# PV with V stationary and two heads on array columns, denominators from added chunks of P, gate logits in the output transposes, deeper page loads

## The chip, the cores and the metric

The kernel runs on one core of a Trainium2 chip. The metric is device time in microseconds (us) of one execution; lower is better. The engines are TensorE (PE, with its weight loads listed apart as PEld), VectorE (DVE), ScalarE (ACT), GpSimd (POOL) and SyncE (SP), which here only issues DMA transfers. TensorE multiplies a stationary operand, loaded first, with columns of a moving operand that stream past it; its clock has two levels, 1.2 and 2.4 GHz.

## What is computed

A causal attention in blocks of 64 over 8 batches, 8 heads, 576 positions and head size 64, and then a mixture of experts without dropped tokens: each of the 4608 tokens goes to the one expert of eight with the largest gate logit.

```
scores = q @ k.T / sqrt(64), kept where block(i) >= block(j)       # blocks of 64
attn   = exp(scores - max) / (sum(exp(...)) + 1e-9)
x      = (attn @ v) as [4608 tokens, 512]
logits = x @ w_gate;  e = argmax(logits);  g = softmax(logits)[e]
y      = g * (relu(x @ w1[e]) @ w2[e])          # w1: 512x1024, w2: 1024x512
```

## The kernel before

**Attention.** The 64 heads are worked off as 32 pairs (p; the loop at L361). A pair's q and k are loaded two pairs ahead (`load`, L123, on SP's queue, together with v), cast to fp16 on POOL (`cast`, L143), transposed on PE (`trans`, L151) and copied out by DVE. `scores` (L165) makes the scores transposed, key positions on partitions and query positions along the columns: four chunks of 128 key rows and one of 64, in steps t = 0 to 3, the two heads on the two halves of the array's rows. ACT takes the exponential from PSUM into the fp32 tile `pt`, called P below; POOL clears the corner that the mask excludes (L189, L191).

`attend` (L193) is the product with V, called PV. For each head and each block i of 128 query rows, every chunk c up to i gives one matmul: the 128 columns of P are stationary, and V's 64 columns and a column of ones (65 in all) move. The column of ones gives the softmax's denominator. That is 15 fp32 matmuls per head; each fp32 matmul is two weight loads and two matmul instructions in the trace, so a pair has 60. `normalise` (L210) divides on DVE, POOL casts the result into the fp16 row `x16`; `xtrans` (L233) transposes the fp32 result on PE, DVE copies it, and `logits` (L243) multiplies it with the gate weights `wg`, 8 columns wide; DVE adds the logits of the four pairs of a batch.

After each batch, `route` (L256) picks the expert on DVE, computes a slot for each token and scatters the rows with five indirect DMAs from POOL (L335) into `xsorted`, a DRAM buffer of 43 pages of 128 rows. It has been filled with empty rows by one DMA of 5.5 MB (L352). The experts' weights `wall` come in 16 loads from POOL's queue (`load_weights`, L91).

**Pages.** The second loop (L473) takes page after page: `mload` loads its rows (L415, SP's queue, tile `xs`, four buffers, two pages ahead), `mtx` transposes (L424), `m1` multiplies with w1 (L438), ACT takes the relu, `mth` transposes (L450), `m2` multiplies with w2 (L460), ACT scales (L463), and POOL scatters the rows to the output with an indirect DMA (L464) that reads its indices from `xs`. So a buffer of `xs` is free when that scatter is through.

**Order.** PE and ACT run in the order of the code (`manual_schedule`); for DVE, POOL and SP a scheduler fixes the order when the program is built. Each queue works in its order: an instruction that waits holds up all behind it.

Of the kernel before, what the change touches and what calls it, by code (L numbers as in the profile page):

```python
# [17 lines left out]
ROW = 258  # L18
# [4 lines left out]
def kernel(  # L23
# [37 lines left out]
    wg = consts.tile([128, HP, E], F32)  # L61
    nc.sync.dma_start(out=wg, in_=moe_w_gate.rearrange("(do di) e -> di do e", di=128))
# [27 lines left out]

    def load_weights(n):  # L91
        e, part = n // 2, n % 2
        if part == 0:
            nc.gpsimd.dma_start(
                out=wall[:, e, 0:8, :].rearrange("p (c a) f -> p c (a f)", c=4),
                in_=moe_w1[e].rearrange("(c p) f -> p c f", p=128))
        else:
            nc.gpsimd.dma_start(
                out=wall[:, e, 8:16, :],
                in_=moe_w2[e].rearrange("(c p) d -> p c d", p=128))  # L100

    with tc.tile_pool(name="ld", bufs=2) as ld, \
         tc.tile_pool(name="vp", bufs=1) as vp, \
# [4 lines left out]
         tc.tile_pool(name="s_ps", bufs=4, space=bass.MemoryType.PSUM) as s_ps, \  # L108
         tc.tile_pool(name="o_ps", bufs=2, space=bass.MemoryType.PSUM) as o_ps, \
         tc.tile_pool(name="t_ps", bufs=2, space=bass.MemoryType.PSUM) as t_ps:  # L110
        vts = [vp.tile([128, 5, 2, 65], F32, name=f"v{i}") for i in range(3)]
        for t in vts:
            nc.gpsimd.memset(t[:, :, :, 64:65], 1.0)
        xTs = [vp.tile([128, 640], F32, name=f"xT{i}") for i in range(2)]
        for t in xTs:
            nc.gpsimd.memset(t[:, 576:640], 0.0)
        ohs = [vp.tile([128, 5, E], F16, name=f"oh{i}") for i in range(2)]
# [5 lines left out]
        def load(p):  # L123
            b, h0 = p // HP, 2 * (p % HP)
            qk = ld.tile([128, 2, 5, 128], F32, name="qk32")
            vt = vts[p % 3]
            for n, src in ((0, q), (1, k)):
                for h in range(2):
                    nc.sync.dma_start(
                        out=qk[:, n, 0:4, h * 64:h * 64 + 64],  # L130
                        in_=src[b, h0 + h, 0:512, :].rearrange("(c p) d -> p c d", p=128))
                nc.sync.dma_start(
                    out=qk[0:64, n, 4, :].rearrange("p (h d) -> p h d", h=2),
                    in_=src[b, h0:h0 + 2, 512:576, :].rearrange("h p d -> p h d"))
            for h in range(2):
                nc.sync.dma_start(
                    out=vt[:, 0:4, h, 0:64],
                    in_=v[b, h0 + h, 0:512, :].rearrange("(c p) d -> p c d", p=128))
                nc.sync.dma_start(out=vt[h * 64:h * 64 + 64, 4, h, 0:64],
                                  in_=v[b, h0 + h, 512:576, :])  # L140
            st["qk", p] = qk

        def cast(p):  # L143
            qk = st.pop(("qk", p))
            h16 = c16.tile([128, 2, 5, 128], F16, name="qk16")
            nc.gpsimd.tensor_copy(h16[:, :, 0:4, :].rearrange("p n c d -> p n (c d)"),  # L146
                                  qk[:, :, 0:4, :].rearrange("p n c d -> p n (c d)"))
            nc.gpsimd.tensor_copy(h16[0:64, :, 4, :], qk[0:64, :, 4, :])
            st["qk16", p] = h16

        def trans(p, n):  # L151
            h16 = st["qk16", p]
            if n == 0:
                st["qkT", p] = c16.tile([128, 2, 576], F16, name="qkT")
            ps = t_ps.tile([128, 576], F16, name="tp")
            for c in range(4):
                nc.tensor.transpose(ps[:, c * 128:c * 128 + 128], h16[:, n, c, :], ident16)  # L157
            nc.tensor.transpose(ps[:, 512:576], h16[0:64, n, 4, :], ident16[0:64, 0:64])
            nc.vector.tensor_copy(st["qkT", p][:, n, :], ps)  # L159


        SC = (((0, 0, 0, 512),), ((1, 0, 128, 448), (0, 448, 512, 64)),
              ((2, 0, 256, 320), (3, 320, 384, 192)))

        def scores(p, t):  # L165
            qkT = st["qkT", p]
            if t == 0:
                st["pt", p] = ptp.tile([128, 2 * 1536 + 64], F32, name="pt")
            pt = st["pt", p]
            if t == 3:  # L170
                sp = s_ps.tile([128, 64], F32, name="s")
                for h in range(2):
                    r = slice(h * 64, h * 64 + 64)
                    nc.tensor.matmul(out=sp[r, :], lhsT=qkT[r, 1, 512:576],
                                     rhs=qkT[r, 0, 512:576], start=True, stop=True)
                nc.scalar.activation(pt[:, 3072:3136], sp, AF.Exp, scale=scale)
                return
            sps = [s_ps.tile([128, 512], F32, name="s") for _ in range(2)]
            for n, (c, o, q0, w) in enumerate(SC[t]):
                for h in range(2):  # L180
                    r = slice(h * 64, h * 64 + 64)
                    nc.tensor.matmul(out=sps[h][:, o:o + w],  # L182
                                     lhsT=qkT[r, 1, c * 128:c * 128 + 128],
                                     rhs=qkT[r, 0, q0:q0 + w], start=True, stop=True)
            for h in range(2):
                o = h * 1536 + t * 512
                nc.scalar.activation(pt[:, o:o + 512], sps[h], AF.Exp, scale=scale)  # L187
            two = pt[64:128, 0:3072].rearrange("p (h w) -> p h w", h=2)
            nc.gpsimd.memset(two[:, :, t * 512:t * 512 + 64], 0.0)  # L189
            if t == 2:  # L190
                nc.gpsimd.memset(two[:, :, 1344:1408], 0.0)  # L191

        def attend(p, h, i):  # L193
            pt, vt = st["pt", p], vts[p % 3]
            if i == 0:
                st["o", p, h] = o_ps.tile([128, 5, 65], F32, name="o")
            o = st["o", p, h]
            m = 128 if i < 4 else 64
            for c in range(i + 1):
                if c == 4:  # L200
                    r, col = slice(h * 64, h * 64 + 64), 3072
                else:
                    r = slice(0, 128)
# [310 lines left out]
```

## Time and profile before

| what | us |
|---|---|
| median of 3 runs (1133.26 to 1137.33) | 1134.91 |
| the profiled execution | 1133.68 |
| its span, first to last instruction | 1131.9 |
| PE busy | 855.7 |
| PE's weight loads busy | 621.7 |
| DVE, ACT, POOL busy | 197.3, 187.8, 193.3 |

The span is the time between the first and the last instruction of the profiled execution; 1.8 us of its time lie outside. Busy times are sums over stages that differ, and a busy PE is not PE at full rate: matmuls overlap, and their rows say how long each was in the array. PE does half its busy time in one line, L206, the product with V. In the second part, the pages, PE is busy for 251 of 424 us.

### The profile page before, as it was taken

What the parts mean: (1) busy time and instruction counts of PE and PEld (TensorE: products, weight loads), DVE (VectorE), ACT (ScalarE), POOL (GpSimd) and SP (SyncE); (2) the same over time, 40 slices, a digit from 0 to 9 for tenths busy, and PEclk for the clock granted to TensorE, in tenths of its full rate; (3) what the DMA queues carried; (4) which work ended last, traced back from release to release, by engine and by line L of the source; (5) the groups of instructions that cost most, each with busy time, mean ns of one, the idle gap of its engine ahead of it and who ended that gap; (6) DMA issues with size and microseconds to landing.
All of it is one profiled execution on the core that took longest, in us unless ns stands there. A gap on an engine that the chain in (4) does not pass through costs nothing. (4 is left out here: it accounts for less than half of the span.)

```text
span 1131.9 us, 12146 instructions
## 1 busy us (share of the span) xinstructions
PE 855.7 (76%) x4357; PEld 621.7 (55%) x4357; DVE 197.3 (17%) x769; ACT 187.8 (17%) x319; POOL 193.3 (17%) x392
## 2 busy tenths in 40 slices
PE   2319999999999999999999991655566555566555
PEld 1217888787888888887878791332232222232222
DVE  0001132131131221311311312111011110111110
ACT  1001121111111121211111100211111111111111
POOL 3112223122122121221131211001110011110011
PEclk9999999999999999999999999988888888888778
DMA  9999952222222121222220000111111111100110
GB/s 186 232 205 186 159 101 69 57 64 63 55 52 70 37 66 45 54 62 49 57 49 17 20 8 28 32 37 42 38 38 33 38 42 43 41 33 31 42 41 5
DMA packets 145785, 71.46 MB, mean 63 GB/s; under 512 B 118976, under 2 KB 138176, under 8 KB 145728
## 3 DMA queue, kind: packets, MB, share of 16 engines
q1 hardware_dynamic: 127952, 39.71, 15.3%
q0 software_dynamic: 17776, 30.98, 12.3%
q8 instruction: 37, 0.61, 0.2%
q14 instruction: 20, 0.16, 0.0%
HBM read 67.56 MB, written 21.71 MB: 79 GB/s over the span
## 5 line engine op out<-in xcount | busy, mean ns | idle before, releaser
L206 PE MATMUL o<-v,pt 128*128 128x65 f32 (+2 forms) x1920 | 399.8, 391 | 0.0
L206 PEld LDWEIGHTS o<-v,pt 128*128 128x128 f32 (+2 forms) x1920 | 360.9, 292 | 56.3 <-issue 33.8
L187 ACT ACTIVATE pt<-s 128x512 f32<-128x512 f32 x192 | 104.0, 595 | 419.8 <-PE s L182 419.8
L424 PE MATMUL xps<-ident,xs 128*128 128x128 f16 x172 | 19.5, 244 | 178.9 <-DMA xs<-xsorted 159.6
L460 PE MATMUL yp<-wall,hT 128*128 x344 | 132.7, 557 | 0.0
L424 PEld LDWEIGHTS <-xs 128*128 128x128 f16 x172 | 11.3, 106 | 199.4 <-DMA xs<-xsorted 197.4
L464 POOL DMA_INDIRECT out_dram<-y,xs x43 | 42.3, 985 | 379.4 <-ACT y L463 377.6
L438 PE MATMUL hp<-wall,xsT 128*128 x344 | 87.2, 399 | 2.6 <-DVE xsT L427 2.6
L157 PE MATMUL tp<-ident,qk 128*128 128x128 f16 x256 | 39.0, 308 | 63.0 <-POOL qk L146 63.0
L427 DVE COPY xsT<-xps 128x512 f16<-128x512 f16 x43 | 18.3, 425 | 366.1 <-PE xps L424 366.1
L460 PEld LDWEIGHTS <-hT 128*128 128x128 f16 x344 | 45.0, 136 | 62.2 <-issue 55.5
L463 ACT ACTIVATE y<-yp,xs 128x512 f32<-128x512 f32 x43 | 29.6, 687 | 285.1 <-PE yp L460 285.1
L182 PE MATMUL s<-qkT 64*128 64x512 f16 (+4 forms) x320 | 63.9, 447 | 16.2 <-DVE qkT L159 15.9
L248 PEld LDWEIGHTS tp<-wg,xT 128*128 128x128 f32 x320 | 72.1, 333 | 0.7 <-DVE xT L238 0.7
L248 PE MATMUL tp<-wg,xT 128*128 128x8 f32 x320 | 71.9, 357 | 0.5 <-DVE xT L238 0.5
L219 DVE RECIPROCAL rec<-o 128x4 f32<-128x4 f32 (+1 forms) x128 | 21.3, 166 | 290.5 <-PE o L206 290.5
L146 POOL CAST qk<-qk 128x1024 f16<-128x1024 f32 x32 | 33.2, 1037 | 197.4 <-issue 140.4
L438 PEld LDWEIGHTS <-xsT 128*128 128x128 f16 x344 | 36.3, 106 | 53.4 <-issue 20.0
L157 PEld LDWEIGHTS <-qk 128*128 128x128 f16 x256 | 22.2, 132 | 68.8 <-POOL qk L146 63.3
L443 ACT ACTIVATE h<-hp 128x1024 f16<-128x1024 f32 x43 | 44.0, 1024 | 78.9 <-PE hp L438 78.9
L189 POOL MEMSET pt<- 64x128 f32 x96 | 19.2, 201 | 215.9 <-ACT pt L187 214.5
L335 POOL DMA_INDIRECT xsorted<-x,slot x40 | 39.0, 974 | 33.1 <-DMA xsorted<-x,slot 17.2
(95 smaller groups left out, 460.7 us busy)
## 6 DMA issues: line engine op xcount, KB each, us to landing
wall<-in_moe_w_dram POOLq DMA_DIRECT2D x16, 1024.0 KB, 13.0
qk<-in_q_dram SPq DMA_DIRECT2D x64, 128.0 KB, 2.6
qk<-in_k_dram SPq DMA_DIRECT2D x64, 128.0 KB, 2.8
v<-in_v_dram SPq DMA_DIRECT2D x64, 128.0 KB, 2.3
xsorted<-fill SPq DMA_DIRECT2D x1, 5547.0 KB, 52.0
xs<-xsorted SPq DMA_DIRECT2D x43, 129.0 KB, 2.0
qk<-in_q_dram SPq DMA_DIRECT2D x32, 32.0 KB, 2.4
qk<-in_k_dram SPq DMA_DIRECT2D x32, 32.0 KB, 2.5
```

What stands on the lines that cost most here:

```text
L146: nc.gpsimd.tensor_copy(h16[:, :, 0:4, :].rearrange("p n c d -> p n (c d)"), qk[:, :, 0:4, :].rearrange("p n c d -> p n (c d)"))
L157: nc.tensor.transpose(ps[:, c * 128:c * 128 + 128], h16[:, n, c, :], ident16)
L182: nc.tensor.matmul(out=sps[h][:, o:o + w], lhsT=qkT[r, 1, c * 128:c * 128 + 128], rhs=qkT[r, 0, q0:q0 + w], start=True, stop=True)
L187: nc.scalar.activation(pt[:, o:o + 512], sps[h], AF.Exp, scale=scale)
L206: nc.tensor.matmul(out=o[0:m, i, :], lhsT=pt[r, col:col + m], rhs=vt[r, c, h, :], start=(c == 0), stop=(c == i), skip_group_check=True)
L248: nc.tensor.matmul(out=lp[:, i * E:i * E + E], lhsT=xT[:, i * 128:i * 128 + 128], rhs=wg[:, hp, :], start=True, stop=True)
L335: nc.gpsimd.indirect_dma_start(out=xsorted[:, :], out_offset=bass.IndirectOffsetOnAxis(ap=slot[0:m, j:j + 1], axis=0), in_=x16[0:m, j, :], ...
L424: nc.tensor.transpose(ps[:, c * 128:c * 128 + 128], pg["xs", T].bitcast(F16)[:, c * 128:c * 128 + 128], ident16)
L438: nc.tensor.matmul(out=hp[:, half * 512:half * 512 + 512], lhsT=xT[:, c * 128:c * 128 + 128], rhs=weight(T, 2 * c + half), start=(c == 0), ...
L443: nc.scalar.activation(h, hp, AF.Relu)
L460: nc.tensor.matmul(out=yp, lhsT=hT[:, f * 128:f * 128 + 128], rhs=weight(T, 8 + f), start=(f == 0), stop=(f == 7))
L464: nc.gpsimd.indirect_dma_start(out=out[:, :], out_offset=bass.IndirectOffsetOnAxis(ap=xs[:, 257:258], axis=0), in_=y, in_offset=None, boun ...
```

## The change

PV is turned round. `attend` now holds a chunk of V (128 keys by 64) and lets P move, in two column ranges of the query positions, 0 to 255 and 256 to 575. The result is transposed: head 0's 64 output dimensions on PSUM partitions 0 to 63, head 1's on 64 to 127, so the two heads' products use the left and the right half of the array's columns. A pair has 14 such matmuls (28 instructions); DVE copies the two ranges into `oT`.

The column of ones is gone. `sums` adds the chunks of P on POOL into `acc`, five adds per pair; `denominators` multiplies 32 columns of ones with P's first 128 columns and with `acc`, each result on its own 32 partitions, and DVE copies them into `den` in four pieces.

`finish` replaces `xtrans`, `logits` and POOL's casts: with a 128-column block of `oT` stationary, one matmul against `wgi`, an identity with the gate weights beside it (144 columns), gives the transposed output and the gate logits; five small matmuls with `den` stationary turn the denominators. DVE divides both straight into `x16` and a logits tile that `route` sums. `finish` for a pair runs one pass later, so the loop has one pass more.

Loads of q and k become two DMAs of 1 KB pieces instead of four of 256 B pieces; v is loaded one pair ahead; the fill of the empty rows is cut into eight pieces, one per batch (12 pages first, then 4 or 5). In the pages, `xs` gets eight buffers and the loads run four pages ahead. In PSUM the scores take two tiles of two banks instead of four of one, and ACT's exponential covers both heads at once. The fp16 tile `qk16` has one buffer instead of two.

```diff
-                nc.tensor.matmul(out=o[0:m, i, :], lhsT=pt[r, col:col + m],
-                                 rhs=vt[r, c, h, :], start=(c == 0), stop=(c == i),
-                                 skip_group_check=True)
...
+        def sums(p):
+
+            pt, p4 = st["pt", p]
+            acc = op.tile([128, 2, 448], F32, name="acc")
+            nc.gpsimd.tensor_tensor(out=acc, in0=pt[:, :, 128:576], in1=pt[:, :, 576:1024],
+                                    op=ALU.add)
+            nc.gpsimd.tensor_tensor(out=acc[:, :, 128:448], in0=acc[:, :, 128:448],
+                                    in1=pt[:, :, 1024:1344], op=ALU.add)
+            nc.gpsimd.tensor_tensor(out=acc[:, :, 256:448], in0=acc[:, :, 256:448],
+                                    in1=pt[:, :, 1344:1536], op=ALU.add)
...
+        def attend(p, cs, half):
...
+            lo, hi = ((0, 256), (256, 576))[half]
...
+            for c in cs:
+                q0 = max(lo, 128 * c)
+                for h in range(2):
+                    r = slice(0, 128) if c < 4 else slice(h * 64, h * 64 + 64)
+                    src = p4[r, :] if c == 4 else \
+                        pt[:, h, COL[c] + q0 - 128 * c:COL[c] + hi - 128 * c]
+                    nc.tensor.matmul(out=o[h * 64:h * 64 + 64, q0 - lo:hi - lo],
+                                     lhsT=vt[r, c, h, :], rhs=src,
+                                     start=(c == 0), stop=(c == last), skip_group_check=True)
+            if cs[-1] == last:
+                nc.vector.tensor_copy(oTs[p % 2][:, lo:hi], st.pop(("o", p, half)))
+
+        def denominators(p):
...
+            ps = t_ps.tile([128, 320], F32, name="tp")
+            for part in range(2):
+                for h in range(2):
+                    r = slice(h * 64, h * 64 + 32)
+                    src = acc[:, h, 0:128] if part else pt[:, h, 0:128]
+                    nc.tensor.matmul(out=ps[r, part * 128:part * 128 + 128], lhsT=ones32,
+                                     rhs=src, start=True, stop=True, skip_group_check=True)
+                    if part == 0:
+                        r = slice(h * 64 + 32, h * 64 + 64)
+                        nc.tensor.matmul(out=ps[r, :], lhsT=ones32, rhs=acc[:, h, 128:448],
+                                         start=True, stop=True, skip_group_check=True)
...
+        def finish(p, part):
...
+            if part == 0:
+                for i in range(5):
+                    col = (i if i < 2 else i - 2) * 128
+                    nc.tensor.matmul(out=ps[:, 432 + 2 * i:434 + 2 * i],
+                                     lhsT=den[:, col:col + 128], rhs=sel[:, int(i > 1), :],
+                                     start=True, stop=True, skip_group_check=True)
+            for m, i in enumerate(ids):
+                nc.tensor.matmul(out=ps[:, m * 144:m * 144 + 144],
+                                 lhsT=oT[:, i * 128:i * 128 + 128], rhs=wgi[:, hp, :],
+                                 start=True, stop=True, skip_group_check=True)
...
-    with tc.tile_pool(name="xs", bufs=4) as xsp, \
+    with tc.tile_pool(name="xs", bufs=8) as xsp, \
...
-                if T + 2 < NP:
-                    mload(T + 2)
+                if T + 4 < NP:
+                    mload(T + 4)
```

On PE, the pass of one pair. Before, from its first PV group to its fp32 transposes (`o` is PV's result, `x_2300` the divided output):

```order
L206 MATMUL o<-v_134,pt 128x65 x6
L182 LDWEIGHTS qkT
L182 MATMUL s<-qkT 128x448
...
L182 MATMUL s<-qkT 128x64
L206 MATMUL o<-v_134,pt 128x65 x4
L206 MATMUL o<-v_134,pt 64x65 x5
L237 MATMUL tp<-ident_64,x_2300 128x128 x4
```

Now, from the start of a pass to the first half of `finish` (L271 and L275 are `denominators`, L258 PV, L300 and L304 `finish`; `den_160` and `oT_156` belong to the pair before):

```order
L271 MATMUL tp<-pt,ones_80 32x128
L275 MATMUL tp<-acc,ones_80 32x320
...
L220 MATMUL s<-qkT 128x512
L258 MATMUL o_1524<-pt,v 64x256 x2
L258 MATMUL o_1524<-pt,v 64x128 x2
...
L258 MATMUL o_1541<-pt,v 64x320 x4
L300 MATMUL tp<-sel,den_160 128x2 x5
L304 MATMUL tp<-wgi,oT_156 128x144 x3
```

A pass now opens with the denominators of the pair before, which read `acc`; many narrow PV products have become few wide ones.

On POOL, one pass between two batches. Before (`qk_2222` is the fp16 cast, `x_1935` the fp16 output row):

```order
L146 CAST qk_2222<-qk_2134 128x2x512
L230 CAST x_1935<-x_1867 128x4x128
L231 CAST x_1935<-x_1867 64x128
L148 CAST qk_2222<-qk_2134 64x2x128
L189 MEMSET pt 64x2x64 x2
```

Now:

```order
L177 CAST qk_1940<-qk_1896 128x2x4x64 x2
L179 CAST qk_1940<-tl_1897 64x2x128
L231 TENSOR_TENSOR acc<-pt 128x896
L233 TENSOR_TENSOR acc<-acc,pt 128x2x320
L225 MEMSET pt 64x2x64
L235 TENSOR_TENSOR acc<-acc,pt 128x2x192
L239 TENSOR_TENSOR acc<-acc,p_1735 64x64 x2
```

The casts of the output are gone, and five adds stand behind the casts of q and k.

On SP, the transfers around the fill. Before, ahead of the third pair's load:

```order
L136 DMA v_134<-in_v_dram 128x4x64
L139 DMA v_134<-in_v_dram 64x64
L352 DMA xsorted<-fill 128x43x258
L129 DMA qk_239<-in_q_dram 128x4x64 x2
L132 DMA qk_239<-in_q_dram 64x2x64
```

Now, where the first piece stands, behind the load of the fourth pair (`qk_342`):

```order
L155 DMA qk_342<-in_k_dram 128x2x256
L158 DMA tl_343<-in_k_dram 64x2x64
L112 DMA xsorted<-fill 128x12x258
L167 DMA v<-in_v_dram 128x4x64
L170 DMA v<-in_v_dram 64x64
```

The fill has moved behind two more pairs' loads of q and k, and its first piece is 12 of 43 pages; the v that follows it is the third pair's.

## Rows read from the trace of the kernel before

**Rows 1.** The page: TensorE's granted clock in 40 slices, in tenths.

```profile
PEclk9999999999999999999999999988888888888778
```

**Rows 2.** Windows by stage: busy us of each engine (instructions), clock, DMA share, GB/s.

```profile
0.00:85.80 85.80, 20.77 (x116) 15.22 (x116) 4.54 (x15) 7.92 (x15) 17.70 (x56) 1.00 1.04 207
85.80:666.30 580.50, 566.26 (x2953) 474.10 (x2953) 136.62 (x620) 106.05 (x217) 127.67 (x287) 1.00 0.31 65
666.30:707.80 41.50, 17.56 (x88) 15.38 (x88) 8.09 (x49) 0.24 (x1) 5.62 (x7) 1.00 0.07 21
707.80:1131.90 424.10, 251.10 (x1204) 117.00 (x1204) 48.01 (x86) 73.60 (x86) 42.34 (x43) 0.83 0.11 36
```

**Rows 3.** Timeline of PE, one pass: start, length, line, operands, count, [idle before <- releaser].

```profile
317.89 0.61 PE L182 MATMUL s<-qkT 64*128 64x512 f16 x2 [0.30 <-DVE qkT L159]
318.43 2.82 PE L206 MATMUL o<-v,pt 128*128 128x65 f32 x12
...
325.09 1.12 PE L237 MATMUL tp<-ident,x 128*128 128x128 f32 x4
...
326.15 0.78 PE L182 MATMUL s<-qkT 64*128 64x320 f16 x4
326.86 2.82 PE L206 MATMUL o<-v,pt 128*128 128x65 f32 x12
329.48 2.24 PE L248 MATMUL tp<-wg,xT 128*128 128x8 f32 x10
331.65 0.26 PE L174 MATMUL s<-qkT 64*64 64x64 f16 x2
331.84 0.61 PE L157 MATMUL tp<-ident,qk 128*128 128x128 f16 x4
...
332.55 3.43 PE L206 MATMUL o<-v,pt 128*128 128x65 f32 x18
...
337.24 0.61 PE L182 MATMUL s<-qkT 64*128 64x512 f16 x2 [0.55 <-DVE qkT L159]
```

**Rows 4.** Timeline of PE: the first pages and the last products.

```profile
710.40 3.57 PE L438 MATMUL hp<-wall,xsT 128*128 x8 [1.01 <-DVE xsT L427]
...
718.53 1.89 PE L438 MATMUL hp<-wall,xsT 128*128 x8 [0.57 <-DVE xsT L427]
...
720.48 0.61 PE L450 MATMUL hps<-ident,h 128*128 128x128 f16 x8
...
722.65 1.89 PE L438 MATMUL hp<-wall,xsT 128*128 x8
...
1118.51 3.62 PE L460 MATMUL yp<-wall,hT 128*128 x16
```

**Rows 5.** Start-up: three rows of the timeline, and the fill's landing time (last number).

```profile
21.18 38.92 SPq L129 DMA_DIRECT2D qk<-in_q_dram  x2
...
26.80 0.61 PE L182 MATMUL s<-qkT 64*128 64x512 f16 x2 [0.55 <-DVE qkT L159]
...
80.40 0.61 PE L157 MATMUL tp<-ident,qk 128*128 128x128 f16 x4 [42.86 <-POOL qk L146]
...
xsorted<-fill SPq DMA_DIRECT2D x1, 5547.0 KB, 52.0
```

**Rows 6.** SP's own waits: line <- what it waited for: us in total, times, longest.

```profile
SPq L415 <- DMA out_dram<-y,xs: 385.8, 39, 18.8
```

**Rows 7.** Groups by line from 85.80 to 666.30 us: busy us, mean ns | idle before.

```profile
L238 DVE COPY xT<-tp 128x512 f32<-128x512 f32 x30 | 20.8, 692 | 8.1 <-PE tp L237 8.1
L220 DVE TENSOR_TENSOR x<-o,rec 128x256 f32<-128x256 f32 x60 | 25.2, 420 | 3.9
L335 POOL DMA_INDIRECT xsorted<-x,slot x35 | 34.2, 977 | 14.7 <-DMA xsorted<-x,slot 8.3 <-issue 6.5
L146 POOL CAST qk<-qk 128x1024 f16<-128x1024 f32 x29 | 30.1, 1037 | 140.9 <-issue 140.4
L189 POOL MEMSET pt<- 64x128 f32 x90 | 18.1, 201 | 207.9 <-ACT pt L187 206.6
```

More of the change, by code (lines that the diff above doesn't have):

```diff
@@ L60 @@
     nc.gpsimd.memset(ones16, 1.0)
-    wg = consts.tile([128, HP, E], F32)
-    nc.sync.dma_start(out=wg, in_=moe_w_gate.rearrange("(do di) e -> di do e", di=128))
+    ones32 = consts.tile([128, 32], F32)
+    nc.gpsimd.memset(ones32, 1.0)
+    wgi = consts.tile([128, HP, 144], F32)
+    nc.gpsimd.memset(wgi, 0.0)
+    for hp in range(HP):
+        nc.gpsimd.tensor_copy(wgi[:, hp, 0:128], ident32)
+        for h in range(2):
+            nc.sync.dma_start(
+                out=wgi[h * 64:h * 64 + 64, hp, 128 + h * E:128 + h * E + E],
+                in_=moe_w_gate[hp * 128 + h * 64:hp * 128 + h * 64 + 64, :])
+    sel = consts.tile([128, 2, 2], F32)
+    for half in range(2):
+        for h in range(2):
+            r = h * 64 + half * 32
+            nc.gpsimd.tensor_copy(sel[:, half, h:h + 1], ident32[:, r:r + 1])
     ione = consts.tile([128, E], F32)
@@ L210, in normalise @@
[L210 to L224 removed]
+            nc.scalar.activation(pt[:, :, t * 512:t * 512 + 512], sp, AF.Exp, scale=scale)
@@ new lines, in scores @@
+            for c in {0: (0,), 1: (1,), 2: (2, 3)}[t]:
+                nc.gpsimd.memset(pt[64:128, :, COL[c]:COL[c] + 64], 0.0)
+        def sums(p):
+            pt, p4 = st["pt", p]
+            acc = op.tile([128, 2, 448], F32, name="acc")
[5 more added lines that the diff above has]
+                                    in1=pt[:, :, 1344:1536], op=ALU.add)
+            for h in range(2):
+                r = slice(h * 64, h * 64 + 64)
+                nc.gpsimd.tensor_tensor(out=acc[r, h, 384:448], in0=acc[r, h, 384:448],
+                                        in1=p4[r, :], op=ALU.add)
+            st["acc", p] = acc
@@ new lines, in attend @@
+        def attend(p, cs, half):
+            pt, p4 = st["pt", p]
+            vt = st["v", p]
+            lo, hi = ((0, 256), (256, 576))[half]
+            if cs[0] == 0:
+                st["o", p, half] = o_ps.tile([128, hi - lo], F32, name=f"o{half}")
+            o = st["o", p, half]
+            last = (1, 4)[half]
+            for c in cs:
+                q0 = max(lo, 128 * c)
+                for h in range(2):
+                    r = slice(0, 128) if c < 4 else slice(h * 64, h * 64 + 64)
[6 more added lines that the diff above has]
+                nc.vector.tensor_copy(oTs[p % 2][:, lo:hi], st.pop(("o", p, half)))
@@ L243, in logits @@
[L243 to L254 removed]
+                    st["lg", b] = op.tile([128, 5, H, E], F32, name="lgp")
@@ L351 @@
             load(1)
-            nc.sync.dma_start(out=xs_pages, in_=fill.unsqueeze(1).to_broadcast([128, NP, ROW]))
+            load_v(0)
             cast(0)
```

230 lines of the change are left out of this document (110 added, 120 removed).

## The prediction

> **What bounds the kernel now.** I read the stages first [rows 2]: 85.8 us of start-up, 580.5 us of attention at a steady pace, 41.5 us until the first page, and 424.1 us of pages. PE is busy nearly all of the second stage, a quarter of the first and 59% of the last.
>
> In the attention one pass takes 19.35 us (scores to scores, 317.89 to 337.24) with only the 0.55 us before the last row idle [rows 3]. PE bounds it. PV takes two groups of 12 instructions and two of 18, 2.82 and 3.43 us, 12.5 us in all: about 0.21 us for an instruction that moves only 65 columns. The gate products are as slow with 8 columns: ten in 2.17 us, from 329.48 to 331.65. So neither is set by its columns, but by loading 128 fp32 columns of weights.
>
> The clock is the trap. The page gives it as full for the whole attention [rows 1], and so does its window [rows 2]. The paces say otherwise. Eight fp16 products of 512 columns take 3.57 us at 710.40 and 1.89 us at 718.53, and the attention's four fp16 transposes (331.84) take as long, 0.61 us, as eight at 720.48 [rows 3, 4]. So the attention runs at 1.2 GHz throughout; PE rose to 2.4 GHz only after eight wide products in a row.
>
> In the pages SP spends 385.8 us waiting for the scatter of an older page before it may load the next [rows 6]. While loaded pages were at hand, a page took 4.12 us (718.53 to 722.65) [rows 4]. Later pages take 10: 424.1 us for 43.
>
> The start-up has one hole of 42.86 us, in which PE waits for POOL's cast; SP had stood for 38.92 us at issuing the load behind the 5.5 MB fill, which took 52.0 us to land [rows 5].
>
> **The change, part by part.** *Pages.* Four pages ahead with eight buffers, a load waits for a scatter that lies five passes before its use, not one; the chain of scatter, landing and load, now one pass of 10 us less PE's own work, gets 20 us. Then PE is late last. The first page's product starts 7.6 us after 707.8 in the trace and the third's at 718.53: 10.7 us. 41 more pages at 4.12 are 169. The last two products follow (some 4 us), and the trace has 9.8 us from the end of its last product (1118.51 + 3.62) to its end [rows 2, 4]. Together 193 instead of 424. ACT, DVE and POOL stay within 4.12 us: 73.6, 48.0 and 42.3 us for 43 pages are at most 1.7 each.
>
> *PV.* Per head 256 + 128 and 320 + 320 + 320 + 192 + 64 = 1600 columns of P move, each in two instructions. No row shows a wide fp32 product. Bounds per column at 1.2 GHz: 0.83 ns as in fp16 (3.57 us for 4096 columns), 1.84 ns by the fp32 transposes (four of 128 columns and one of 64, 1.06 us from 325.09 to the scores) [rows 3, 4]. I take 1.67, near the upper row, which is the same type: 5.3 us per head. If the two heads run side by side, as the row halves do in the scores (two times 512 columns and the change to the next group in 0.54 us, where one after the other takes 0.85), a pass needs 5.3 plus one lone instruction in each of the three groups (0.43, 0.53, 0.53): 6.8 us. One after the other it is 10.7. At 2.4 GHz: 3.4 or 5.3.
>
> The Trainium skill bears on this: *TensorE: Matmul & The Clock Gate*, Part 3, says that products on different column groups run at once, and gives 2.38 times for three of them. No run here shows it for columns; by it the 3.4 stands.
>
> *Denominators.* Six products, 1152 columns, twice: 3.8 us in series, 2.1 side by side in the order of the code; 1.05 at the high clock. DVE's four copies are some 1.8 us (692 ns for 512 columns, 420 for 256 [rows 7]) and lie under the scores and PV that follow; `finish` needs them 3 us later.
>
> *Finish.* Ten instructions set by the weight load (0.214) and ten that move 144 columns (0.24): 4.5 us, or 2.3. It replaces transposes and gate products of 1.1, 0.2 and 2.2 us.
>
> *The rest on PE.* Scores stay: 0.54, 0.54, 0.71 and 0.19, 2.0 us, or 1.2. The transposes of q and k stay: twice 0.71, or 0.75 in all. Nine more changes between kinds of groups at the 0.11 us that a group of scores shows beyond its columns: 1.0. At the seam PE waits for DVE's copy of qkT, 0.30 to 0.55 [rows 3], and the copy is now strided and behind two more DVE operations: 1.1.
>
> Sum of a pass: 3.4 + 1.05 + 2.3 + 1.2 + 0.75 + 1.0 + 1.1 = 10.8 us at 2.4 GHz, and 6.8 + 2.1 + 4.5 + 2.0 + 1.4 + 1.0 + 1.1 = 18.9 at 1.2. Which of them holds decides the time. I expect the high clock: denominators, scores and the first two PV groups are now some 8 us of wide products nearly back to back, what the eight products at 710.40 were; before, 0.21 us of weight load went with every 65 columns. I take **11.2 us**, with 0.4 for stretches at the low clock.
>
> *POOL.* It loses 0.9 us of casts and gains 2048 adds per partition. The nearest row is a cast, 1.0 ns per element with one input [rows 7]: 2.1 us, or with two inputs to read 4.2; I take the latter. With casts (1.04 and a small one, 1.4), clears (four of 0.2) and scatters (five of 0.98 per four passes) a pass is 7.6 us on POOL. The adds wait for PE's denominators of the pair before, and PE waits for them one pass later: cover of some 3 us.
>
> A rule speaks against this edit. The Trainium skill, *GPSIMD Engine Reference*, sections 3.1 and 4.1, calls VectorE the engine for adding tiles and gives 4497 ns for 2048 fp32 elements on GpSimd. No row here shows such an add; by it the pass is 7.9 us on POOL, under 11.2 all the same.
>
> *DVE* has some 6 us per pass, ACT three exponentials of 1024 columns: neither is late.
>
> *Start and end.* The first pass began at 26.80 us [rows 5], held up by its second pair's load among many small pieces; with fewer, larger ones I estimate 17, though POOL has some 3 us more to prepare. The hole of 43 us goes. What comes next: the first piece, 12 of 43 pages, 14.5 us by its share of 52.0, stands ahead of the third pair's v; and 16 loads of weights at 207 GB/s [rows 2] with faster passes. For both 20 us, between 0 and 45. Scatters that hold POOL, whose queue carries the adds: 8. The last stretch has no scores and less PV, but the same routing and five scatters: 35 instead of 41.5.
>
> The sum: 17 + 31 x 11.2 (347) + 20 + 8 + 35 + 193 = 620, and 1.8 outside the span: **622 us**, against 1133.7 for the profiled execution, 1.2 below the median, which changes nothing here.
>
> **Rivals.** *The heads' halves don't overlap* (clock high): PV +1.9, denominators +0.9, 31 x 2.8 = 87: 709 us. For it: no row shows column halves; against it: row halves overlap.
>
> *The clock stays low in the attention.* 31 x 7.7 = 239 and some at the end: 866 us; when half of the passes are low, 745. For it: 600 us of busy PE didn't raise it before, and `finish` is again loads with few columns. Against it: the wide stretches.
>
> *Both at once:* 24.5 us per pass, 1034.
>
> *The pages don't get faster*, because the load waits for something other than the buffer: 853 us. Against it: the wait of SP names the scatter, and the first three pages ran at PE's pace.
>
> *Slower than before:* POOL's adds bound the pass. PE waits at the head of each pass for `acc`, with scores and PV queued behind. The forecast has 512 us to lose, 16.5 per pass: a pass of 27.7, so 24 for the adds, 11.9 ns per element instead of 1.0 for a cast. No row comes near.
>
> **How the numbers follow.** Forecast 0.54; no overlap of halves 0.15 (709); low clock in part 0.13 (745), throughout 0.10 (866); both 0.03 (1034); pages 0.03 (853); POOL's adds 0.02 (slower). The range reaches down to 580 (a pass of 10, no start-up loss) and up to 790, which leaves out about 0.18 above and 0.02 below. A change of 0.3% is about what a measurement can tell from none: faster 0.97, same 0.01, slower 0.02.
>
> **What would show it.** Right: a pass of 10 to 12 us with scores' groups some 0.3 apart; the granted clock's first rise in the first passes; page products every 4.12 us and SP's wait for scatters gone; no hole above 10 us before the third pass. Wrong: second-head products that start when the first head's end; transposes of q and k at 0.61 per four; PE waiting for `acc` at the head of passes.

## The result and the profile after

The changed kernel takes 661.63 us (median of 4 runs, 654.85 to 662.26) against 1134.72 us for the kernel before on the same chip: a ratio of 0.5816, 95% interval 0.5776 to 0.5855. The forecast was 622 us, its range 580 to 790. The profiled execution took 662.26 us, 660.5 of them span.

The windows by stage of the changed kernel answer to [rows 2]: each row is a stretch of the span, in us. Columns: stretch, length, busy us of PE, PEld, DVE, ACT and POOL with instructions, clock, DMA share, GB/s. The stages are the start; passes 0 to 9; the other 21 passes that still have scores; the rest up to the first page; the pages.

```profile
0.00:16.43 16.43, 4.86 (x32) 2.48 (x33) 5.14 (x9) 4.25 (x5) 13.05 (x52) 1.00 0.82 167
16.43:169.30 152.87, 112.58 (x812) 64.10 (x812) 77.46 (x209) 33.47 (x42) 90.50 (x143) 0.81 0.97 189
169.30:425.50 256.20, 212.49 (x1734) 126.78 (x1736) 172.22 (x479) 70.51 (x89) 179.84 (x276) 0.88 0.33 90
425.50:468.30 42.80, 13.74 (x101) 9.14 (x100) 13.03 (x58) 0.24 (x1) 12.74 (x16) 0.66 0.16 49
468.30:660.50 192.20, 179.76 (x1204) 96.74 (x1203) 48.03 (x86) 73.64 (x86) 42.13 (x43) 0.97 0.23 76
```

| stretch | forecast | measured |
|---|---|---|
| before the first pass | 17 | 16.4 |
| 31 passes with scores (347 + 20 for the start + 8 for scatters) | 375 | 409.1 |
| last stretch | 35 | 42.8 |
| pages | 193 | 192.2 |
| outside the span | 1.8 | 1.8 |

So all of the miss lies in the attention, 34 us in its passes and 8 behind them. The clock line of the page, where [rows 1] stood at 9 for the whole attention, now says that the clock moves:

```profile
PEclk9997867796797998887998888975699999999998
```

The timeline of PE in one pass without a long wait answers to [rows 3] (start, length, line, operands, count, [idle before <- releaser]):

```profile
241.58 0.27 PE L271 MATMUL tp<-pt,ones 128*32 128x128 f32 x1 [0.35 <-DVE lgp L317]
...
242.71 0.39 PE L220 MATMUL s<-qkT 64*128 64x512 f16 x2 [0.39 <-DVE qkT L193]
243.03 0.87 PE L258 MATMUL o<-pt,v 128*64 128x256 f32 x8
243.83 0.39 PE L220 MATMUL s<-qkT 64*128 64x64 f16 x4
244.15 1.30 PE L258 MATMUL o<-pt,v 128*64 128x320 f32 x8
245.38 1.28 PE L300 MATMUL tp<-sel,den 128*128 128x2 f32 x10
246.52 0.98 PE L304 MATMUL tp<-wgi,oT 128*128 128x144 f32 x6
247.43 0.39 PE L220 MATMUL s<-qkT 64*128 64x320 f16 x4
247.76 0.40 PE L189 MATMUL tp<-ident,qk 128*128 128x128 f16 x4
...
248.22 1.08 PE L258 MATMUL o<-pt,v 128*64 128x320 f32 x8
...
249.39 0.20 PE L213 MATMUL s<-qkT 64*64 64x64 f16 x2
249.52 0.76 PE L304 MATMUL tp<-wgi,oT 128*128 128x144 f32 x4
250.11 0.39 PE L189 MATMUL tp<-ident,qk 128*128 128x128 f16 x4
```

Scores' groups start 0.32 us before the next kind, and four fp16 transposes take 0.40 instead of 0.61: this is the higher of the two levels, 2.4 GHz. PV is 0.80 + 1.23 + 1.17 = 3.2 us (start to start of what follows), `finish` 1.14 + 0.91 + 0.59. With the seam (the two short waits for DVE in brackets, 0.35 and 0.39 us) such a pass is 9.4 us, shorter than the 10.8 of the forecast; but the mean of the 31 is 13.2. The difference begins with PE's waits, here of the whole kernel (engine, line, what was waited for: us in total, times, longest):

```profile
PE tp L358 <- DVE oh L355: 25.6, 8, 3.3
PE tp L275 <- POOL acc L239: 19.5, 10, 3.9
PE xps L494 <- issue: 19.4, 1, 19.4
PE tp L191 <- POOL qk L179: 13.3, 6, 6.7
PE tp L300 <- DVE den L280: 12.7, 8, 2.1
```

The routing's one-hot (`oh`, the 0/1 row that marks each token's expert), POOL's sums, POOL's casts and the denominators' copies stand in the attention; 19.4 us are the one wait for the first page. Behind most of these waits some microseconds run at the low clock. Behind one wait for `acc`, shown here, the scores' row that was 0.39 is 0.55, and the granted clock from 282.1 to 285.5 us is 0.50:

```profile
281.37 0.46 PE L275 MATMUL tp<-acc,ones 128*32 128x320 f32 x1 [1.85 <-POOL acc L239]
...
282.02 0.55 PE L220 MATMUL s<-qkT 64*128 64x512 f16 x2
```

Not behind all of them: after waits for `acc` of 1.80 us (from 189.04) and 1.73 us (from 328.79) the granted clock stayed at 1.00.

### The profile page after: what moved, and what is told of

Same layout as the page of the kernel before. It is cut to its first block, busy times and chain, and to the rows that moved or that the text cites. A ratio compares the mean times of both kernels' runs of the same rounds, so it can differ in the third digit from the quotient of the medians.

```text
span 660.5 us, 11179 instructions
## 1 busy us (share of the span) xinstructions
PE 523.4 (79%) x3877; PEld 299.3 (45%) x3877; DVE 315.9 (48%) x841; ACT 182.1 (28%) x223; POOL 338.3 (51%) x529
## 5 line engine op out<-in xcount | busy, mean ns | idle before, releaser
L223 ACT ACTIVATE pt<-s 128x1024 f32<-128x1024 f32 x96 | 98.2, 1025 | 238.4 <-PE s L220 216.4
L258 PE MATMUL o<-pt,v 128*64 128x320 f32 (+3 forms) x768 | 130.2, 469 | 3.1 <-DMA v<-in_v_dram 3.1
L193 DVE COPY qkT<-tp 128x512 f16<-128x512 f16 x64 | 82.9, 1299 | 29.6 <-PE tp L191 29.5
L258 PEld LDWEIGHTS o<-pt,v 128*64 128x64 f32 x768 | 56.2, 164 | 55.9 <-issue 36.0
L530 PE MATMUL yp<-wall,hT 128*128 x344 | 81.1, 379 | 0.0
L231 POOL TENSOR_TENSOR acc<-pt 128x896 f32<-128x896 f32 x32 | 66.7, 2084 | 22.1 <-PE tp L271 21.5
L403 POOL DMA_INDIRECT xsorted<-x,slot x40 | 39.5, 986 | 65.7 <-DMA xsorted<-x,slot 15.1
L280 DVE COPY den<-tp 32x256 f32<-32x256 f32 (+1 forms) x128 | 57.8, 451 | 31.2 <-PE tp L271 29.0
L304 PE MATMUL tp<-wgi,oT 128*128 128x144 f32 x320 | 64.7, 341 | 0.0
L300 PEld LDWEIGHTS tp<-sel,den 128*128 128x128 f32 x320 | 41.2, 204 | 29.6 <-issue 29.6
L177 POOL CAST qk<-qk 128x512 f16<-128x512 f32 x64 | 37.8, 612 | 31.8 <-issue 14.2
L508 PEld LDWEIGHTS <-xsT 128*128 128x128 f16 x344 | 34.0, 99 | 43.8 <-issue 2.9
L300 PE MATMUL tp<-sel,den 128*128 128x2 f32 x320 | 43.7, 262 | 12.7 <-DVE den L280 12.7
L304 PEld LDWEIGHTS tp<-wgi,oT 128*128 128x128 f32 x320 | 50.6, 220 | 2.3
L233 POOL TENSOR_TENSOR acc<-acc,pt 128x640 f32<-128x640 f32 x32 | 49.3, 1539 | 1.3
L275 PE MATMUL tp<-acc,ones 128*32 128x320 f32 x128 | 33.9, 493 | 19.5 <-POOL acc L239 19.5
## 6 DMA issues: line engine op xcount, KB each, us to landing
wall<-in_moe_w_dram POOLq DMA_DIRECT2D x16, 1024.0 KB, 11.2
```

Source lines behind the costliest of these rows:

```text
L193: nc.vector.tensor_copy(qkT[:, n, 0:512].rearrange("d (p c) -> d c p", c=4), ps[:, 0:512].rearrange("d (c p) -> d c p", c=4))
L223: nc.scalar.activation(pt[:, :, t * 512:t * 512 + 512], sp, AF.Exp, scale=scale)
L231: nc.gpsimd.tensor_tensor(out=acc, in0=pt[:, :, 128:576], in1=pt[:, :, 576:1024], op=ALU.add)
L233: nc.gpsimd.tensor_tensor(out=acc[:, :, 128:448], in0=acc[:, :, 128:448], in1=pt[:, :, 1024:1344], op=ALU.add)
L258: nc.tensor.matmul(out=o[h * 64:h * 64 + 64, q0 - lo:hi - lo], lhsT=vt[r, c, h, :], rhs=src, start=(c == 0), stop=(c == last), skip_group_ ...
L280: nc.vector.tensor_copy(den[r:r + 32, 0:w], ps[r:r + 32, 0:w])
```

## The experiments

The times are medians; the columns by stage are of one profiled execution each. "Passes" run from scores to scores, "last" from the scores of the last such pass to the first page's transposes, which includes that pass. Lines added ahead of a place raise its number: L275 of the changed kernel is L277 in e7, c2 and c3. The runs come from several chips, so the ratio is to the kernel before on the same chip.

| kernel | us | ratio to before (95%) | passes 0-9 | 10-29 | last | pages |
|---|---|---|---|---|---|---|
| changed | 661.6 | 0.5816 (0.5776-0.5855) | 15.3 | 12.45 | 49.9 | 192 |
| e1 pages only | 902.6 | 0.7959 (0.7946-0.7973) | | | | 192 |
| e2 attention only | 887.0 | 0.7833 (0.7796-0.7870) | 14.9 | 12.5 | 47.9 | 421 |
| e3 heads in series | 672.7 | 0.5938 (0.5917-0.5959) | 15.3 | 13.0 | 47.6 | 192 |
| e7 weights late | 647.5 | 0.5702 (0.5690-0.5715) | 12.3 | 13.1 | 52.6 | 194 |
| e8 last scatter only | 633.5 | 0.5590 (0.5571-0.5609) | 14.2 | 11.6 | 45.4 | 192 |
| e4 sums on DVE | 629.7 | 0.5561 (0.5536-0.5586) | 15.1 | 11.1 | 44.0 | 192 |
| e6 route later | 657.8 | 0.5803 (0.5773-0.5833) | 15.0 | 12.2 | 52.8 | 192 |
| e9 route at the end | 683.2 | 0.5998 (0.5962-0.6034) | 14.7 | 13.4 | 57.3 | 194 |
| e5 copy in order | 653.6 | 0.5776 (0.5748-0.5804) | 15.0 | 11.9 | 48.6 | 194 |
| c1 = e4 + e5 + short copies | 602.4 | 0.5309 (0.5290-0.5327) | 14.7 | 10.3 | 42.8 | 192 |
| c2 = c1 + e7 | 587.3 | 0.5185 (0.5165-0.5204) | 11.0 | 11.2 | 43.8 | 194 |
| c3 = c2 + e9 | 546.9 | 0.4835 (0.4815-0.4855) | 9.9 | 9.8 | 42.6 | 192 |

**The two halves of the change, each alone.** e1 puts only this on the kernel before, with four pages loaded ahead of the loop; e2 takes only this from the changed one:

```
-    with tc.tile_pool(name="xs", bufs=4) as xsp, \
+    with tc.tile_pool(name="xs", bufs=8) as xsp, \
...
-                if T + 2 < NP:
-                    mload(T + 2)
+                if T + 4 < NP:
+                    mload(T + 4)
```

> Only the deeper page loads (8 buffers, four loads ahead) on top of the kernel before; its attention is untouched. If the pages took 424 us there because the transfers came late and the clock was at 1.2 GHz in consequence, the pages alone should take about 192 us as in the changed kernel, and the whole 1134.9 - 231 = 904 us (885 to 925). Rival: the pages became fast because the attention of the changed kernel leaves the scatters and the fill landed earlier or the clock up when they start; then this run keeps pages of 8 to 9 us and stays above 1050.

> The changed kernel with the page loads of before (4 buffers, two loads ahead). If the two parts of the change add up, 661.6 + 231 = 893 us (870 to 915), with the first page at about 468 us as in the changed kernel. Rival: the page loads' depth matters only with the old attention; then about 665 us.

The pages alone bring 1133.6 - 902.6 = 231 us, the attention alone 1133.6 - 887.0 = 247, together 478; the whole change brought 473. So the halves add up, to 5 us. SP's own waits in e2 show what held the pages, as [rows 6] did:

```profile
SPq L485 <- DMA out_dram<-y,xs: 385.6, 39, 20.7
```

With eight buffers the same line still stands, but ahead of need:

```profile
SPq L485 <- DMA out_dram<-y,xs: 145.8, 35, 17.8
```

SP waits 145.8 us there and no page is late for it: page products start every 4.12 us from the third page on. The forecast's "wait gone" was wrong in the word; it was its place on the path that went.

**Do the two heads run side by side?**

```
-            for c in cs:
-                q0 = max(lo, 128 * c)
-                for h in range(2):
+            for h in range(2):
+                for c in cs:
+                    q0 = max(lo, 128 * c)
```

> In every call of attend the chunks of head 0 are multiplied first and then those of head 1, so that matmuls on different column halves no longer alternate. If the two heads' matmuls run at the same time only where they stand next to each other, PV goes from 3.2 us to nearer 6 of a pass at 2.4 GHz, and 31 passes give 60 to 95 us: about 720 to 755 us. If PE takes instructions far enough ahead to overlap them anyway, or if they never overlapped, it stays within 10 us of 661.6.

PE's timeline of a pass of e3:

```profile
223.28 0.88 PE L258 MATMUL o<-pt,v 128*64 128x256 f32 x8
224.09 0.39 PE L220 MATMUL s<-qkT 64*128 64x64 f16 x4
224.42 1.30 PE L258 MATMUL o<-pt,v 128*64 128x320 f32 x8
225.65 1.28 PE L300 MATMUL tp<-sel,den 128*128 128x2 f32 x10
...
228.49 1.08 PE L258 MATMUL o<-pt,v 128*64 128x320 f32 x4
229.49 0.33 PE L258 MATMUL o<-p,v 64*64 64x64 f32 x2
229.75 1.08 PE L258 MATMUL o<-pt,v 128*64 128x320 f32 x4
...
231.04 0.39 PE L304 MATMUL tp<-wgi,oT 128*128 128x144 f32 x1
```

The third group shows the overlap by its absence: the second head starts at 229.75, when the first is through, and the group takes 2.5 us instead of 1.17. In the first two groups, where two products of one head stand ahead of the other's, nothing changed (0.81 and 1.23 us): there PE still ran both heads at once. So the halves overlap, and the rival without overlap was false. The run also shows what more work on PE costs here: 1.36 us times 31 passes are 42 us, of which 14 arrived at the end (0.0122 of 1134). In passes 0 to 29 PE's idle time fell from 84.0 to 71.5 us and its clock rose from 0.85 to 0.88, which makes up for the rest: the mean pass isn't bound by PE's work alone.

**The early passes.** In the changed kernel the 16 weight loads are issued between 7.4 and 154.5 us, and the DMA engines are busy for 0.97 of passes 0 to 9. e7 ties each to a pass, by

```
+        if n:
+            nc.gpsimd.tensor_copy(wall[:, e, 8 * part, 0:1], st["acc", 2 * n - 1][:, 0, 0:1])
```

> Each of the later 15 weight loads is made to wait for the sums of a pass (a copy of one element a partition from that pass's acc into the region that the load fills goes ahead of it), so that the loads come one in every two passes and no longer nearly all in the first ten. Theory: in the changed kernel the passes 0 to 9 take 15.3 us each against 12.45 later because the weight transfers fill the DMA engines and q, k and v come late; then these passes fall to about 12.5 us, -28 us in all: 630 to 640 us. Rival: the early passes are long for another reason (the first loads, the fill, a low clock after waits); then they stay at 15 us and the time within 5 us of 661.6. Second rival: the loads only move their trouble to the later passes, which get 1 us longer each.

Windows of e7, passes 0 to 9 and 10 to 29:

```profile
16.42:139.16 122.74, 100.41 (x812) 58.90 (x813) 77.52 (x209) 33.42 (x42) 82.28 (x137) 0.87 0.69 149
139.16:400.83 261.67, 207.32 (x1673) 121.12 (x1672) 169.08 (x470) 67.10 (x85) 182.74 (x290) 0.88 0.59 128
```

The first ten passes fall by 30 us, as the theory said, at a DMA share of 0.69. But the later twenty rise from 249.1 to 261.7, the last stretch by 3, and the net is 13 us (0.0114 of 1134). Both the theory and the second rival hold, each for its stretch. Whether the later passes pay for the transfers themselves or for POOL's part in issuing them, no run separates: PE's waits for `acc` there rose from 9.7 to 18.8 us.

**POOL: scatters and sums.** e8 leaves out the scatters of batches 0 to 6 (first edit); e4 moves all adds of `sums` from POOL to DVE (the second, and so for the others).

```
-            for j in range(5):
+            for j in range(5 if b == B - 1 else 0):
...
-            nc.gpsimd.tensor_tensor(out=acc, in0=pt[:, :, 128:576], in1=pt[:, :, 576:1024],
+            nc.vector.tensor_tensor(out=acc, in0=pt[:, :, 128:576], in1=pt[:, :, 576:1024],
```

> Leaves out the scatters of the token rows of the first seven batches; only the last batch's five scatters are issued, so the rows of the others never reach the sorted pages. All matmuls and the routing's arithmetic stay. Theory: the scatters hold POOL (35 issues of 0.99 us and the waits of one for the landing of the other), and POOL's sums come late for TensorE; the waits of the sums' last add for a scatter (24 us, 8 times) then vanish and the passes after a batch's end shorten by 2 to 4 us each: 635 to 645 us. Rival: the scatters stand in gaps of POOL and the long passes of every fourth come from the routing's wait of TensorE for the one-hot (23 us) alone; then 655 to 662.

> All five adds of the sums go from POOL to VectorE. Theory: POOL is what sets the passes above 9.4 us (its adds take 5.3 us and stand behind the scatters); on VectorE they are an estimated 2.4 us (by the product's row, 0.49 us for 384 elements, about 1.2 ns an element), and the passes shorten to 10.5 to 11.5 us: 600 to 630 us. Rival: VectorE, with about 7.3 us of work in a pass already and in line with the sums, becomes the bound: the pass is 12 us or more and the time 650 to 690 us. A part of either would leave it between 630 and 650.

Without the scatters the time falls by 26 us, with the sums elsewhere by 29, and PE's waits for `acc` vanish in both. Its waits for the denominators' copies stay without the scatters (11.8 us for 12.7) and nearly go with the sums on DVE (2.3). POOL's timeline in the changed kernel, behind a batch's routing, shows how the two meet:

```profile
276.91 1.01 POOL L403 DMA_INDIRECT xsorted<-x,slot  x1 [0.16 <-issue]
277.95 0.34 POOL L239 TENSOR_TENSOR acc<-acc,p 64x64 f32<-64x64 f32 x1
281.00 0.32 POOL L239 TENSOR_TENSOR acc<-acc,p 64x64 f32<-64x64 f32 x1 [2.71 <-DMA xsorted<-x,slot]
```

The second half of the last add waits 2.71 us for the landing of a scatter, and PE's denominators (281.37) with it. The forecast had the scatters' issues in POOL's 7.6 us and 8 us more for the scatters' hold of the queue; that the wait for a landing can stand in POOL's queue ahead of the pass's last add, as here, it did not have. In the last stretch, where nothing else is on POOL, five scatters stand 2.98 us apart, 0.96 of it issue. An estimate from these rows: POOL needs 5.3 us of adds, 1.6 of casts and 0.8 of clears per pass, four times, and five times 2.98 per batch, 45.7 us for four passes; PE needs 4 x 9.4 = 37.6. Four passes took 49.8 (4 x 12.45). The scatters aren't all of it: without them four passes still took 46.3 (4 x 11.57).

With the sums on DVE the short passes are 9.8 us, and the two around each batch's end 12 to 13. The adds there take 1.16, 0.82, 0.52 and twice 0.22 us, 2.9 instead of the 2.4 I had estimated.

**The routing.** PE waits 3 us for the one-hot at each batch's end, and the routing's matmuls need it. e6 splits `route` behind the one-hot and writes the matmuls and all that follows after `attend(p, (0, 1), 1)` of the next pass; e9 writes them ahead of `scores(p + 1, 3)` there.

```
+                if p > 1 and p % HP == 1 and now:
+                    route_tail(p // HP - 1)
```

> The routing's matmuls and all behind them are written a third of a pass later, between the second and the third part of the next pass, where VectorE's one-hot is long ready; the first VectorE steps stay where they are. Theory: TensorE's wait of 3.3 us for the one-hot, 7 times, is on the path and goes: 638 to 645 us. Rival: TensorE then meets the sums or the scatters' hold of POOL at the same place, and no more than 8 us come back.

> The changed kernel with nothing but the routing's matmuls moved to the end of the next pass (the earlier try put them a third of a pass on and kept the wait of 3 us). In the last combination this same step brought 40 us, with the sums on VectorE. Theory A: what the routing costs is TensorE's wait for the one-hot and the low clock behind it, whatever engine does the sums; then about 5 us for each of seven batches come back here too, 620 to 632 us. Theory B: with the sums on POOL the scatters still hold them, and POOL takes the wait's place; then 645 to 662 us. That A and B each own a half would give about 640.

e6 did nothing that can be told from the spread, since PE waits there too:

```profile
PE tp L362 <- DVE oh L355: 23.4, 8, 3.8
```

DVE was not idle ahead of that one-hot. Its steps stand between the denominators' four copies, and two of them (40 elements a partition, 0.20 us each in the changed kernel) are long:

```profile
203.96 2.18 DVE L343 TENSOR_TENSOR d<-lg,mx 128x40 f32<-128x40 f32 x1
...
206.62 1.12 DVE L348 SCALAR_TENSOR_TENSOR val<-d,pref 128x40 f32<-128x40 f32 x1
```

They end at 206.14 and 207.74, where POOL's first two adds end at 206.08 and 207.69. (The expectation of c3 puts this wait down to a copy that itself waited for TensorE; these rows show no such wait.) PE's waits moved besides: those for `acc` fell from 19.5 to 4.3 us, those for POOL's last cast rose from 13.3 to 35.5.

e9 removed the wait (one of 2.6 us is left, the last batch's) and became 21 us slower: passes 10 to 29 lost 19 and the last stretch 7, while the first ten gained 6. Neither of its theories foresaw that. PE's waits in e9:

```profile
PE tp L300 <- DVE den L280: 41.1, 16, 4.5
...
PE tp L275 <- POOL acc L239: 8.1, 6, 2.0
```

The sums aren't late; the copies of the denominators are. DVE's timeline there, and POOL's at the same time:

```profile
270.42 1.67 DVE L383 TENSOR_TENSOR new<-pages,pages 128x8 f32<-128x8 f32 x1
...
272.12 1.60 DVE L384 TENSOR_TENSOR_SCAN inc<-ione,used,new 128x8 f32<-128x8 f32 x1
273.64 0.40 DVE L280 COPY den<-tp 32x256 f32<-32x256 f32 x1
273.97 0.83 DVE L385 TENSOR_TENSOR base<-inc,new 128x8 f32<-128x8 f32 x1
```

```profile
269.98 2.08 POOL L231 TENSOR_TENSOR acc<-pt 128x896 f32<-128x896 f32 x1 [0.25 <-PE tp L271]
272.14 1.54 POOL L233 TENSOR_TENSOR acc<-acc,pt 128x640 f32<-128x640 f32 x1
273.77 1.01 POOL L235 TENSOR_TENSOR acc<-acc,pt 128x384 f32<-128x384 f32 x1
```

Routing steps on 8 elements take 1.67, 1.60 and 0.83 us. They end at 272.09, 273.72 and 274.80, and POOL's three adds end at 272.06, 273.68 and 274.78: each step ends within 0.04 us of the add beside which it stood. The copy from PSUM (0.40 us, and 0.41 on average in e4, where no add is on POOL) isn't held. The denominators' copies are queued between these steps, and PE's `finish` waits for the copies. Moving the matmuls put the steps where the next pass's copies are due.

**DVE, and all together.** e5 turns the order of the copy; c1 adds e4 and fewer copies of the denominators:

```
-            nc.vector.tensor_copy(qkT[:, n, 0:512].rearrange("d (p c) -> d c p", c=4),
-                                  ps[:, 0:512].rearrange("d (c p) -> d c p", c=4))
+            nc.vector.tensor_copy(qkT[:, n, 0:512].rearrange("d (p c) -> d p c", c=4),
+                                  ps[:, 0:512].rearrange("d (c p) -> d p c", c=4))
...
-            for r in range(0, 128, 32):
-                w = 320 if r % 64 else 256
-                nc.vector.tensor_copy(den[r:r + 32, 0:w], ps[r:r + 32, 0:w])
+            nc.vector.tensor_copy(den[:, 0:256], ps[:, 0:256])
+            for r in (32, 96):
+                nc.vector.tensor_copy(den[r:r + 32, 256:320], ps[r:r + 32, 256:320])
```

> The copy of the transposed q and k writes its 512 columns in order and reads PSUM with a stride, where the changed kernel writes with a stride of four elements (1299 ns each, two a pass). If the strided write is what makes it slow, the copy falls to 0.5 to 0.8 us. As VectorE stands on the chain of a pass (denominators' copies, reciprocal, products, these copies), theory 1 expects 0.5 to 1 us a pass back: 630 to 648 us. Theory 2, that POOL and TensorE set the pass and VectorE has slack: the copy gets faster and the time stays within 5 us. If the strided read costs as much as the strided write, nothing moves.

> The sums on VectorE, the copy of transposed q and k written in order, and the four copies of the denominators (0.45 us each) as one copy of 128x256 and two of 32x64: VectorE loses about 1.2 us by the one and 1.0 us by the other in a pass and gains 2.2 by the sums. Theory: with the sums on VectorE its line of steps is what lengthens the passes of 12 to 13 us, so the total falls by another 0.3 to 1 us a pass, to 600 to 620 us. Rival: TensorE's own work (9.8 us in the short passes) and the routing's wait for the one-hot set all passes by then; the total stays within 6 us of 629.7.

The copy's group in the changed kernel and in e5 (busy us, mean ns | idle before, from 28 to 434 us):

```profile
L193 DVE COPY qkT<-tp 128x512 f16<-128x512 f16 x60 | 77.9, 1299 | 22.1 <-PE tp L191 22.0
```

```profile
L193 DVE COPY qkT<-tp 128x512 f16<-128x512 f16 x60 | 41.0, 684 | 26.1 <-PE tp L191 25.9
```

It was the strided write. Alone, this gives 4.5 us by the ratios (0.0040 of 1134), which can't be told from the spread: the intervals of e5 and of the changed kernel overlap. With the sums on DVE the same copy and the shorter denominators bring 27 us (c1 against e4). What an edit of DVE is worth depends on who is late.

> As c1, and the weight loads spread over the passes. With the sums alone on VectorE the passes 0 to 9 took 15.1 us and TensorE waited 20 us for v there. Theory: the early passes fall to about 11 us and the later ones stay, since POOL, which the spreading burdens, no longer does the sums: 35 us less than c1, 570 to 590 us. Rival, from the run with the weight loads late alone: 13 us come back in later passes; then 585 to 605.

> As c2, and the routing's matmuls and all behind them come at the end of the next pass, some 8 us after the one-hot was asked for (the earlier try put them a third of a pass later, where VectorE stood behind a copy that itself waited for TensorE, and the wait stayed at 3 us). Theory: TensorE no longer waits 7 times 3.3 us there and the clock doesn't fall in consequence: 20 to 30 us under c2. Rival: the wait only takes the place of others in the same pass (for v, the scores' eviction, the denominators), and under 8 us come back.

c2 is 15 us under c1: the early passes give 37, the later ones take 18 back, as in e7. c3 then brings 40, more than the 20 to 30 expected, by the very step that cost 21 in e9. In c3 the sums are on DVE, the step `new` takes 0.15 us on average and PE waits 0.6 us in all for the denominators. That the place of the sums decides it is argued from these rows: c3 and e9 also differ in the copies and in the weight loads, and no run changes the sums' place alone there. In c2 PE waits 22.3 us for the one-hot (8 times, the longest 2.8), and in c3 one wait of 2.9 us is left. So 19 us of this wait went, and 40 us of time. Windows of passes 10 to 29 of c2, then of c3:

```profile
124.04:347.45 223.41, 191.83 (x1672) 118.66 (x1671) 174.41 (x550) 67.08 (x85) 88.18 (x189) 0.91 0.70 149
```

```profile
113.79:309.10 195.31, 178.05 (x1670) 111.07 (x1671) 174.80 (x553) 66.04 (x85) 101.26 (x187) 0.99 0.78 170
```

Of the 28.1 us between them, 14.3 were idle time of PE. The other 13.8 are busy time with the same work, at a clock of 0.99 instead of 0.91: the low clock behind the waits. PE's waits for POOL's casts (15.6 us in c2) went too, so that not all of it is the one-hot's. c3, at 546.9 us, beats the changed kernel by 17% and the kernel before by 52%; a pass without routing takes 9.0 us in it, PE's own work and the seam.

## Why the forecast was near, and where its steps were off

**Pages: right.** 193 forecast, 192.2 measured, and e1 and e2 show that this half stands alone.

**PV and the clock: right in kind.** The passes ran mostly at the high clock (0.81, then 0.88), the heads overlap (e3), and PV took 3.2 us for 3.4. The rivals of no overlap, of a clock that stays low, of slow pages and of a slower kernel fell.

**The undisturbed pass: too long by 1.4 us.** 9.4 instead of 10.8: denominators some 0.7 for 1.05, the seam 0.74 for 1.1, and no extra 1.0 for changes between groups, against 0.35 more for `finish`.

**The passes' mean: the step that failed.** The forecast let PE bound the pass (11.2 us) and put DVE and POOL beside it, because each one's busy time was below it. It added 8 us for scatters, gave POOL's adds a cover of some 3 us, and had no term for the one-hot. Passes 10 to 29 took 12.45, 3 us more than PE's 9.4, or 61 in all. PE's waits there are 16.4 us for the one-hot, 9.7 for `acc` and 8.5 for the denominators (five of each, 34.6 together); the other 26 are by this sum PE's own work, made longer by a mean clock of 0.88. Three causes stand behind the waits, and the runs separate them only in part: POOL's sums behind the landing of scatters (26 us of the whole time by e8), the one-hot (38 us of passes between c2 and c3 with its low clock, but only where the sums are out of the way), and the DVE steps that POOL's adds hold (e4 takes these away together with the first, 29 us). How much of the time each owns in the changed kernel itself stays open, since they overlap: e9 took one away and lost.

**Luck.** That 622 came within 40 us of 661.6 is in part luck. 31 undisturbed passes of 9.4 are 291 us where the forecast had 347; what came on top of them was 118 us where it had 28. Of its signs of being right, the pass of 10 to 12 us did not come (13.2), and one of being wrong did: PE waited for `acc` at the head of passes.

**The adds: mis-sized.** 4.2 us forecast, 5.3 measured (2.08, 1.54, 1.00 and twice 0.32); the three larger ones are 2.4 ns an element, 4.62 us for 1920. The Trainium skill, *GPSIMD Engine Reference*, section 3.1, gave 4497 ns for 2048 elements; the measured times are above that too, so its figure was the nearer one, and still low. The forecast set it aside since 7.9 us on POOL lay under 11.2. POOL was in fact busy for 8.6 us a pass (179.84 in 21 passes), below the pass as well; its queue, not its busy time, was what mattered.

**DVE: mis-sized.** Some 6 us a pass forecast, 8.2 measured (172.22 in 21 passes, routing included). The copies of qkT are 1.30 us each, for 0.46 in the kernel before; alone they cost little by e5.

**The start: mis-sized.** 20 us allowed; passes 0 to 9 took 152.9, 41 above ten times 11.2. e7 shows 30 of it to come from the weights' loads.

**The last stretch:** 42.8 for 35. The wait for the first page, with the five scatters in it, is 19.4 us, as in the kernel before (19.3). So what stands ahead of it took 23.3 us, as long as there (23.2): less PV on PE brought nothing. PE waits 9.6 us in it for the sums, the denominators and the routing, and the whole stretch had a clock of 0.66.

**Two readings.** The prediction has the first page's product 7.6 us after 707.8; by its own row, 710.40, it is 2.6, which the sum doesn't use. Its 0.83 ns a column is 0.87 by the row that it cites (3.57 us for 4096 columns).

## What to carry to other kernels

An engine whose busy time is below the pass can still set it: add up its queue with the landings that an in-order instruction awaits, not only the work. Between c2 and c3 TensorE's short waits cost their length and about as much again at the low clock behind them (14.3 and 13.8 us), so a wait of 3 us per batch can be worth an edit that looks idle. Moving a step off the path pays only when no other engine stands ready to be late there; e9 lost 21 us, and the same edit, with the sums on VectorE and three more edits, won 40.

## What the runs showed of the hardware that I had not expected

- A VectorE step of 8 elements a partition, 0.15 to 0.23 us in e4, can take 0.8 to 1.8 us beside a POOL add and then ends with it; the profile counts this as busy time and not as a wait. The group of L377 shows it, first in the changed kernel and then in e4, with the adds on VectorE:

```profile
L377 DVE TENSOR_SCALAR pages<-pages 128x8 f32<-128x8 f32 x8 | 11.2, 1394 | 0.0
```

```profile
L377 DVE TENSOR_SCALAR pages<-pages 128x8 f32<-128x8 f32 x8 | 1.2, 152 | 0.0
```

  The Trainium skill, *SBUF — State Buffer*, section "SBUF: two separate sides", says that VectorE and GpSimd share one pair of ports as an exclusive lock, held for a whole instruction, when the VectorE step has two SBUF inputs or runs in a two-port mode. The ends of the three steps of e9, within 0.04 us of the adds' ends, agree, and so does the unheld copy from PSUM. L377 has one SBUF input, so by that sentence it would have to run in a two-port mode; no run shows which mode it ran in.
- A VectorE copy from PSUM of 512 fp16 elements a partition that writes with a stride of four takes 1299 ns; written in order and read with a stride, 684.
- TensorE ran the second head's products beside the first's even with two products of the first ahead of them (0.81 us for the group), and not in the group of three (2.5 us instead of 1.17). The third product there also has another shape, 64 rows, and no run separates its shape from the count.
